# Softmaxes, waiting copies and a DMA queue put in another order: top-k attention and a GELU MLP on one Trainium2 core

## The chip, the cores and the metric
The kernel runs on one core of one Trainium2 chip. The metric is the device time of one execution in microseconds (us), and less is better. The profiles show the core's engines: PE (matmul, with its weight loads as PEld), DVE (vector), ACT (scalar), POOL and SP, whose queue issues the transfers spoken of here. Each engine runs its own instructions in program order.

## The reference
Attention with only the 32 largest scores of each row kept, then an MLP with exact GELU, all in float32.

```python
# q, k, v: 8 batches, 8 heads, 576 rows, 64 dims
scores = 1 / sqrt(64) * q @ k.T
kth    = 32nd largest of each row
scores = where(scores >= kth, scores, -1e9)
scores = scores - max(scores)
attn   = exp(scores); attn = attn / (sum(attn) + 1e-9)
x      = (attn @ v), heads side by side       # 4608 x 512
out    = gelu_exact(x @ w_in) @ w_out         # 512 x 2048, 2048 x 512
```

## The kernel before
The attention is cut into 144 *items*, 18 for each batch. Two heads make a pair, four pairs a batch. A main item is one pair and one tile of 128 rows (four tiles of a pair). The remaining 64 rows of a head go into *last-row items*, each for two pairs. In even batches the two last-row items come at the end of the batch, in odd ones at its start, so that over each two batches four of them follow one another (items 88 to 91, for instance). `starts` holds the first item of each batch.

The main loop has one *slot* n for each item and works on several items at once, in stages. In slot n:

- PE computes scores of item n + 2, and in most even slots those of n + 3 as well (`scores`, L406, L421); ACT copies them out of PSUM (L414, L425).
- DVE finds the 32 largest scores of item n (`top_k`, L502 and L505, after `larger`, L441).
- POOL writes the threshold (`threshold`, L516 and L517), and ACT softmaxes item n - 1: `select`, an activation that pushes scores below the threshold far down (L536), and `softmax`, the exponential with its sum (L548), once for each of the two heads e = 0, 1. Then POOL adds the 1e-9 (`add_small`, L529), DVE inverts (`inverse`, L523), and POOL normalises (L571).
- PE transposes item n - 2 (`transposes`: L371, L385, L647, L661), with ACT's copies of the results (keys: L379, L390; L650; `pt`: L676).
- PE multiplies item n - 3 by v (`attend`, L727, and L738 for last-row items), and `copy_x` lets ACT copy the result into xT (L732, L744).
- PE's pieces of the MLP (`mlp`) fill in: h_ps (L790), in odd slots followed by ACT's two gelus (`run_gelus`, L806, with a table load ahead), and the products with w_out (L944, L946), whose copies ACT makes (L965, L962). Every fourth pair of slots closes a block of 256 tokens, with more copies by ACT (L987 to L1003).

Scores, threshold, softmax and the rest of an item thus run through slots that follow one another, and what each engine does in a slot is set by the order in which the loop calls these functions. In a slot before the change ACT's order is: score copies, then `copy_x` (L1222), then in odd slots the gelus (with the table load ahead and L965 behind them), then `softmax(n - 1, 0)`, the copies of keys and pt, and `softmax(n - 1, 1)`. A call of `softmax` for an item whose `select` was not yet done does that first. The loop's form holds from slot 13 on (`few[0]`), `late` from slot 11.

In PSUM, o, t_ps, tp_t and seven share one bank, s_ps and tp another, and h_ps and the second s_ps a third: PE's next use of a bank follows ACT's copy of the one before.

Some items (`squared`: from 26 on the even ones, and the last-row items but for the very last) are not transposed on PE alone: DVE transposes blocks (`square_p`), SP writes them to DRAM (`write_p`, L605, four DMAs) and reads them back rearranged into pt (`read_p`, L615, four DMAs). A `delayed` item is a squared last-row item. SP's queue carries these writes and reads, the loads of q, k and v (v: L138 and L142) and the stores of y (`run_stores`, L861). It is ordered by hand: while `held[0]` is set, `issue` puts a load off until `flush` at the end of the slot's `write_p`; `soon` holds one that `issue_soon` lets go after a later attend.

Of the kernel before, what the change touches and what calls it, by code (L numbers as in the profile page):

```python
# [14 lines left out]
def kernel(  # L15
# [239 lines left out]
    items, starts = [], []  # L255
# [19 lines left out]
    few = [False]  # L275
# [305 lines left out]
    def delayed(i):  # L581

        return squared(i) and items[i][1] == NM
# [23 lines left out]
    def read_p(i):  # L607

        if squared(i):
            d = turned.pop(i)  # L610
            if i % 2 == 0:
                pt_now[0] = pt_tile()
            cols = slice(i % 2 * P, (i % 2 + 1) * P)
            for k in range(P // SQ):
                nc.sync.dma_start(  # L615
                    out=pt_now[0][k * SQ : (k + 1) * SQ, :, cols], in_=d[:, :, k, :]
                )
# [77 lines left out]
    def copy_x():  # L695
        while copies:
            copies.pop()()
# [10 lines left out]
    def attend(i):  # L708

        if i < 0 or i >= N:  # L710
            return False
        pair, t = items[i]
        b, at = divmod(pair, NP)
        if t < NM and t % 2 == 0:
            return False
        pt = pt_now[0]
        o = bank("o")
        n, row = (2 * P, (t - 1) * P) if t < NM else (TL, SM)
        tok = place_of(b, row)
        gap = RING if t == NM else COLS if tok % RING >= COLS else RING - COLS  # L720
        assert read[0] >= tok - gap + n
        c = slice(column(tok), column(tok) + n)
        if t < NM:
            vt = raw_of("v", pair)
            for j in range(NJ):
                for e in range(2):
                    nc.tensor.matmul(  # L727
                        o[e * D : (e + 1) * D, 0:n], lhsT=vt[:, j, e, :],
                        rhs=pt[:, e * NJ + j if j < NM else NM, :],
                        start=(j == 0), stop=(j == NJ - 1),  # L730
                    )
            copies.append(lambda: nc.scalar.copy(out=xT[:, at, c], in_=o[:, 0:n]))  # L732
        else:
            for r in range(2):
                vt = raw_of("v", pair + r)
                for j in range(NJ):
                    for e in range(2):
                        nc.tensor.matmul(  # L738
                            o[e * D : (e + 1) * D, r * TL : (r + 1) * TL],
                            lhsT=vt[:, j, e, :],  # L740
                            rhs=pt[:, e * NJ + j if j < NM else NM, i % 2 * P :][:, half(r, e)],
                            start=(j == 0), stop=(j == NJ - 1),
                        )
            copies.append(lambda: nc.scalar.copy(  # L744
                out=xT[:, at : at + 2, c],
                in_=o[:, 0 : 2 * TL].rearrange("p (r n) -> p r n", n=TL),
            ))

        if t == (NM if b % 2 == 0 else NM - 1):
            for r in range(2 if t == NM else 1):  # L750
                f = lambda r=r: load("v", pair + r + NP)
                if r == 0 and delayed(i):
                    soon.append(f)
                else:
                    issue(f)
        if at == (NP - 1 if t < NM else NP - 2):
            assert n_tok[0] == tok
            n_tok[0] = tok + n
        return True
# [106 lines left out]
    def run_stores():  # L866
        for f in older:
            f()
        older[:] = stores
        stores.clear()  # L870
# [303 lines left out]
    for n in range(ahead):  # L1174

        held[0] = n < N and squared(n - 2)
        mid = [i for i in (n - 5, n - 4) if delayed(i) and n % 2 and (i % 2 or i in starts)]
        even_last = delayed(n - 4) and n % 2 == 0 and n - 4 not in starts
        if not mid and not even_last:
            read_p(n - 3)  # L1180

        def mids():
            attend(mid.pop(0))
            if not mid:
                copy_x()
                read_p(n - 3)
                issue_soon()
        left[0] = room_in(n)
        few[0] = n > START + 2
        eager[0] = n > N  # L1190
        left[0] += closes(n - 3) - closes(n - 2)
        if not waits(unit_in(n)):
            weights_add(unit_in(n))
        if n > 0:
            larger(n + 1)
        for piece in squares_in.pop(n, []):
            piece()
        if n == 1:

            for e in range(2):  # L1200
                select(0, e)
            for e in range(2):
                softmax(0, e)
        two = few[0] and n % 2 == 0 and n + 3 < N and items[n + 3][1] < NM
        scores(n + 2, two)
        if two:
            scores(n + 3)
        if even_last:
            product = attend(n - 4)
            issue_soon()  # L1210
            read_p(n - 3)
        else:
            product = not delayed(n - 3) and attend(n - 3)
        if len(mid) == 2:
            mids()
        late = n > START
        if n != 1 and n < START:

            for e in range(2):
                select(n - 1, e)  # L1220
            softmax(n - 1, 0)
        copy_x()  # L1222
        if n == START:

            for e in range(2):
                select(n - 1, e)
            softmax(n - 1, 0)
        if waits(unit_in(n)):
            weights_size(unit_in(n))
            weights_add(unit_in(n))  # L1230
        mlp(1)
        if closes(n - 3):
            ready[0] = n_tok[0]
        if few[0] and n % 2:
            run_gelus()
        tr = transposes(n - 2)
        if product and n > START and done[0] < len(pieces) and pieces[done[0]][0] > ready[0]:

            for piece in tr[:1]:
                piece(n + 2 if few[0] else None)  # L1240
            tr, ready[0] = tr[1:], n_tok[0]
        if not few[0] and n > START:
            softmax(n - 1, 0)
        mlp(1)
        if n != 1 and not late:
            softmax(n - 1, 1)
        if few[0]:
            softmax(n - 1, 0)
            if n % 2:
                mlp(ODD)  # L1250
                if mid:
                    mids()
        mlp(1)
        prep = prep_in.pop(n, [])
        if n == 0:
            weights_size(unit_in(1))
            keep_busy(14, ident)
        if n == START + 1:

            for piece in prep:  # L1260
                piece(None)
            prep = []
        if len(prep) > 1 and len(tr) == 3:
            tr, prep = tr[:1] + prep[:1] + tr[1:], prep[1:]
        now = tr[:-1]
        if few[0]:
            now, tr, prep = tr + prep[:1], [], prep[1:]
        for x, piece in enumerate(now):
            piece(n + 2 if few[0] else None)
            ready[0] = n_tok[0]  # L1270
            if few[0] and x == 2:
                break
            mlp(1)
        ready[0] = n_tok[0]
        if late:
            softmax(n - 1, 1)
        if n > 0:
            smaller(n + 1)
        add_small(n - 1)
        for piece in tr[-1:] + prep:  # L1280
            piece(None)
            mlp(1)
        if n < START:

            keep_busy(4 if n == 0 else 8 if product else 14 if n < 5 else 18, ident)

        run_gelus()
        mlp(left[0])
        run_gelus()
        if n < N:  # L1290
            top_k(n, lambda: inverse(n - 1), lambda: square_p(n - 2))
            write_p(n - 2)
            flush()
            if n == 0:
                larger(1)
        else:
            inverse(n - 1)
        threshold(n)
        if n == 0:
            smaller(1)  # L1300
        normalise(n - 1)
        sum_up(n + 2)
        if n in sums_in:
            weight_sums(sums_in[n])
        run_small(6)

        if n > 0 and not waits(unit_in(n + 1)):
            weights_size(unit_in(n + 1))
        run_stores()
        if n == N:  # L1310
            run_stores()
        for m in (n + 1, n + 2):

            if m > 2 and waits(unit_in(m)) == (m == n + 1):
                load_weights(m)
        if n < NP:
            load("v", n)
        if n == 5:
            nc.vector.memset(flat["k"][0][TL:, 0:TL], 0.0)
            load("q", SQUARES)  # L1320
            load("k", SQUARES)
# [38 lines left out]
```

## Time and profile before

| | |
|---|---|
| time, median of 3 runs | 1477.53 us (1476.33 to 1479.15) |
| the profiled execution: its time, its span | 1479.29 us, 1477.5 us |
| granted TensorE clock | 0.999 |
| busy share of the span: PE, PEld, DVE, ACT, POOL | 98%, 77%, 89%, 73%, 77% |
| q1 (all of SP's transfers): MB, share of 16 engines | 124.93, 39.8% |
| writes of turned<-s, reads of pt<-turned | 240 each, 144 KB, 3.5 and 3.2 us to landing |
| loads of v, stores of y | 64 of 128 KB (3.0 us), 30 of 256 KB (2.1 us) |

A line of the timeline gives the start in us from the span's start, the duration, the engine (SPq is SP's DMA queue, at the time of issue), the line of the kernel, the operation, what it writes and reads, and a count; in brackets stands the idle time before it on its engine, and what ended that. A line of the waits gives the engine and line that waited, what it waited for, the us in total, how often, and the longest. A number such as 98% is an average over all stages.

### The profile page before, as it was taken

The page shows a single profiled execution, that of the slowest core. Times are in us where ns is not written, and L with a number is a line of the kernel's source. Part 1 is how long each engine was busy: PE and PEld are TensorE (multiplying, and loading weights), DVE is VectorE, ACT ScalarE, POOL GpSimd, SP SyncE. Part 2 cuts the span into 40 slices and gives each one's busy share as a digit, 9 for nine tenths or more (in the row PEclk, how much of TensorE's full clock was granted, in tenths as well). Part 3 has the DMA queues.
Part 4 walks back from the last instruction along what each step waited for, and adds up shares of the span by engine and source line. Part 5 has one row for each costly group of instructions (what it writes and reads, how often), then busy time and mean ns, then how long its engine had stood idle before and what let it go on. Part 6 is the DMA issues. An engine that isn't in the chain of part 4 may idle for free. (4 is left out here: it accounts for less than half of the span.)

```text
span 1477.5 us, 26521 instructions
## 1 busy us (share of the span) xinstructions
PE 1449.7 (98%) x8693; PEld 1134.6 (77%) x8693; DVE 1307.8 (89%) x3331; ACT 1082.8 (73%) x1902; POOL 1142.0 (77%) x1290
## 2 busy tenths in 40 slices
PE   8999999999999998999999999999999999999999
PEld 6776677887777776888777777787777777787787
DVE  7999899999999999899999999899999999898701
ACT  7999877877777686777777777677777777677620
POOL 6877567878898888777898978787788888887632
PEclk9999999999999999999999999999999999999999
DMA  7425210045435356345534347344543435523300
GB/s 198 144 86 129 78 47 1 24 92 103 93 71 91 67 107 129 65 95 112 102 81 78 74 74 151 76 92 96 99 101 73 89 63 97 125 61 73 68 15 15
DMA packets 544713, 127.04 MB, mean 86 GB/s; under 512 B 466464, under 2 KB 536128, under 8 KB 544576
## 3 DMA queue, kind: packets, MB, share of 16 engines
q1 hardware_dynamic: 543312, 124.93, 39.8%
q8 instruction: 69, 1.13, 0.3%
q14 instruction: 68, 0.56, 0.1%
q10 hardware_dynamic: 1200, 0.39, 0.1%
q0 software_dynamic: 64, 0.03, 0.0%
HBM read 80.47 MB, written 44.83 MB: 85 GB/s over the span
## 5 line engine op out<-in xcount | busy, mean ns | idle before, releaser
L790 PE MATMUL h_ps<-xT,w_in_sb 128*128 128x256 f32 (+1 forms) x2560 | 534.1, 361 | 0.0
L790 PEld LDWEIGHTS h_ps<-xT,w_in_sb 128*128 128x128 f32 x2560 | 437.5, 190 | 73.3 <-issue 25.2
L502 DVE MAX8 top<-lists 128x8 f32<-128x576 f32 (+1 forms) x792 | 475.5, 639 | 0.0
L505 DVE MATCH_REPLACE8 lists<-top,lists 128x288 f32<-128x288 f32 (+1 forms) x528 | 307.6, 588 | 0.0
L571 POOL TENSOR_TENSOR s<-s,stat 128x1152 f32<-128x1152 f32 x135 | 286.1, 2119 | 0.3 <-DVE stat L523 0.3
L536 ACT ACTIVATE s<-s,stat 128x576 f32<-128x576 f32 x288 | 224.7, 788 | 16.6 <-POOL stat L516 16.4
L548 ACT ACTIVATE s<-s,stat 128x576 f32<-128x576 f32 x288 | 224.6, 782 | 11.3 <-POOL lists L466 0.7
L529 POOL TENSOR_SCALAR stat<-stat 128x2 f32<-128x2 f32 x144 | 31.6, 219 | 210.4 <-ACT s L548 183.8
L474 POOL TENSOR_TENSOR lists<-lists 128x576 int32<-128x576 int32 x132 | 186.4, 1412 | 4.0
L466 POOL TENSOR_TENSOR lists<-s 128x576 int32<-128x576 int32 x133 | 188.0, 1413 | 0.0
L727 PE MATMUL o<-pt,raw_v 128*64 128x256 f32 x1280 | 152.9, 384 | 4.3 <-DMA pt<-turned 2.4
L806 ACT ACTIVATE g<-h_ps 128x512 f32<-128x512 f32 x144 | 78.2, 594 | 107.0 <-PE h_ps L790 106.8
L727 PEld LDWEIGHTS o<-pt,raw_v 128*64 128x64 f32 x1280 | 87.9, 136 | 88.3 <-issue 43.1
L946 PE MATMUL y_ps<-w_out_sb,sum 128*128 128x256 f32 x472 | 140.8, 380 | 0.0
L414 ACT ACTIVATE s<-s_ps 128x1024 f32<-128x1024 f32 x127 | 124.9, 1031 | 9.2 <-PE s_ps L406 8.8
L406 PE MATMUL s_ps<-kt,qm 64*128 64x512 f32 x512 | 129.4, 618 | 0.8 <-ACT s L412 0.8
L676 ACT COPY pt<-tp 128x1024 f32<-128x1024 f32 x73 | 74.4, 1019 | 56.2 <-PE tp L661 56.1
L505 DVE MATCH_REPLACE8 lists<-first,lists 128x288 f32<-128x288 f32 x264 | 114.2, 438 | 0.0
L946 PE MATMUL y_ps<-w_out_sb,g 128*128 128x256 f32 x480 | 113.4, 379 | 0.0
L523 DVE RECIPROCAL stat<-stat 128x2 f32<-128x2 f32 x144 | 22.9, 159 | 95.2 <-POOL stat L529 94.4
L502 DVE MAX8 first<-lists 128x8 f32<-128x288 f32 x268 | 106.5, 436 | 0.0
L441 DVE TENSOR_TENSOR lists<-s 128x576 f32<-128x576 f32 x133 | 101.1, 760 | 0.0
(162 smaller groups left out, 2483.3 us busy)
## 6 DMA issues: line engine op xcount, KB each, us to landing
turned<-s SPq DMA_DIRECT2D x240, 144.0 KB, 3.5
pt<-turned SPq DMA_DIRECT2D x240, 144.0 KB, 3.2
raw_v<-in_v_dram SPq DMA_DIRECT2D x64, 128.0 KB, 3.0
raw_q<-in_q_dram SPq DMA_DIRECT2D x112, 72.0 KB, 2.3
raw_k<-in_k_dram SPq DMA_DIRECT2D x112, 72.0 KB, 2.4
out_dram<-y SPq DMA_DIRECT2D x30, 256.0 KB, 2.1
w_out_sb<-in_moe_w_in_dram SPq DMA_DIRECT2D x14, 511.8 KB, 4.8
w_out_sb<-in_moe_w_out_dram SPq DMA_DIRECT2D x10, 511.8 KB, 4.1
```

The source lines that it names most:

```text
L406: nc.tensor.matmul(s_ps[:, e], lhsT=q_t[rows, :], rhs=kt[rows, main_keys(pair)], start=True, stop=True)
L414: nc.scalar.activation(spread(s, S + TL, SM), s_ps, func=AF.Copy, scale=scale)
L466: nc.gpsimd.tensor_tensor(t[:, :, 1].bitcast(i32), a.bitcast(i32), b.bitcast(i32), op=ALU.add)
L474: nc.gpsimd.tensor_tensor(into_of(i)[:, :, 1].bitcast(i32), both, top, op=ALU.subtract)
L502: nc.vector.max(x[:, e], src[:, e])
L505: nc.vector.match_replace(dst[:, e], x[:, e], src[:, e], LOWEST)
L536: nc.scalar.activation(s, s, func=AF.Prelu, bias=st["neg"][:, e : e + 1], scale=1.0, alpha=STEEP)
L548: nc.scalar.activation(s, s, func=AF.Exp, bias=st["bias"][:, e : e + 1], scale=1.0, accum_out=st["den"][:, e : e + 1],)
L571: nc.gpsimd.tensor_tensor(s, s, wide, op=ALU.mult)
L727: nc.tensor.matmul(o[e * D : (e + 1) * D, 0:n], lhsT=vt[:, j, e, :], rhs=pt[:, e * NJ + j if j < NM else NM, :], start=(j == 0), stop=(j = ...
L790: nc.tensor.matmul(h_tile(u)[:, i, :], lhsT=w_in_sb[:, ko, f * P : (f + 1) * P], rhs=xT[:, ko, c0 : c0 + n], start=(ko == 0), stop=(ko == ...
L946: nc.tensor.matmul(acc[names][:, k], lhsT=lhsT, rhs=rhs, start=(j == 0 and k == 0), stop=(j == FT // 2 - 1 and k == 1),)
```

## The change
From slot 13 on:

- In even slots `select(n - 1, 0)`, `softmax(n - 1, 0)` and `select(n - 1, 1)` come ahead of `copy_x`, and `softmax(n - 1, 1)` right behind it.
- In odd slots both selects come ahead of `copy_x` and of the gelus with their table load; both exponentials follow the gelus and L965, ahead of the copies of keys and pt.
- On SP, at the four last-row items, v's first loads behind an odd one of these items are no longer put off through `soon`, and the stores of y of one slot are issued at the next slot's start, behind its reads. At three places in the kernel (near 575, 920 and 1268 us) the order turns from read (4), write (4), four loads of v, two stores of y, read (4), with four loads of v ahead of the write, into read (4), write (4), eight loads of v, read (4), two stores of y.

PE, DVE and POOL run the same instructions in the same order as before; ACT runs the same ones in another order.

```diff
                 f = lambda r=r: load("v", pair + r + NP)
-                if r == 0 and delayed(i):
+                if r == 0 and delayed(i) and i % 2 == 0:
                     soon.append(f)
                 else:
                     issue(f)
...
+        def stores_later(m):
+            return m % 2 == 0 and delayed(m - 3) and m - 4 in starts
+
         even_last = delayed(n - 4) and n % 2 == 0 and n - 4 not in starts
         if not mid and not even_last:
             read_p(n - 3)
+        if stores_later(n):
+            run_stores()
...
+        if few[0]:
+            select(n - 1, 0)
+            if n % 2 == 0:
+                softmax(n - 1, 0)
+            select(n - 1, 1)
         copy_x()
+        if few[0] and n % 2 == 0:
+            softmax(n - 1, 1)
...
         if few[0]:
-            softmax(n - 1, 0)
             if n % 2:
+                softmax(n - 1, 0)
+                softmax(n - 1, 1)
                 mlp(ODD)
                 if mid:
                     mids()
...
-        if late:
+        if late and not few[0]:
             softmax(n - 1, 1)
...
-        run_stores()
+        if not stores_later(n + 1):
+            run_stores()
```

## The prediction
> **What bounds the kernel now.** I read the page first, then the busy times by window, PE's waits, the waits of all engines, and the timeline at the places that the diff touches.
>
> ```profile
> span 1477.5 us, 26521 instructions
> PE 1449.7 (98%) x8693; PEld 1134.6 (77%) x8693; DVE 1307.8 (89%) x3331; ACT 1082.8 (73%) x1902; POOL 1142.0 (77%) x1290
> ```
>
> The profiled execution took 1479.29 us, 1.76 us over the median of 1477.53. All that follows is a difference of times, so I add it to the median. The window is two batches of the regular part (584 to 932 us); its columns are the length and then the busy time of PE, PEld, DVE, ACT, POOL.
>
> ```profile
> 584.00:932.00 348.00, 342.64 (x2041) 269.33 (x2037) 326.30 (x835) 256.61 (x457) 286.99 (x322) 1.00 0.47 93
> ```
>
> PE is the bound, and DVE is close behind: over the 18 pairs of slots in this window DVE has 21.7 us left, 1.2 us a pair. What the change can win is what PE waits for. PE's waits from 120 us on are short: engine, line, releaser, us in total, times, longest.
>
> ```profile
> PE o L738 <- DMA pt<-turned: 5.7, 3, 2.2
> PE o L727 <- DMA pt<-turned: 2.4, 2, 1.9
> PE t_ps L371 <- ACT xT L744: 2.2, 3, 0.7
> PE tp_t L647 <- POOL s L571: 1.5, 4, 0.5
> PE o L727 <- ACT s L548: 1.2, 1, 1.2
> ```
>
> Together 13.0 us, 0.9% of the span: that is all there is to win. What the change visibly acts on lies beside PE:
>
> ```profile
> POOL stat L529 <- ACT s L548: 183.8, 71, 6.0
> ACT g L806 <- PE h_ps L790: 106.8, 52, 11.7
> DVE stat L523 <- POOL stat L529: 94.4, 91, 9.8
> ```
>
> POOL and, through it, DVE wait for ACT's exponentials, while ACT stands at the head of its queue waiting for PE's h_ps. With the selects and exponentials put ahead of those waits, most of the 94.4 us of DVE goes. DVE is not the bound, so this is worth nothing by itself. What it can buy is a lead of the thresholds over PE.
>
> **Part 1: ordinary pairs of slots.** In an odd slot ACT ran gelu's table load, two gelus and the copy L965, then the first select. Now both selects come first, and they need POOL's L516 of the same slot.
>
> ```profile
> 806.63 0.79 POOL L516 TENSOR_SCALAR stat<-top 128x2 f32<-128x2 f32 x1 [0.60 <-DVE stat L523]
> 806.83 1.09 ACT L806 ACTIVATE g<-h_ps 128x512 f32<-128x512 f32 x2 [2.04 <-PE h_ps L790]
> 807.80 0.38 ACT L965 COPY p<-seven 128x256 f32<-128x256 f32 x1
> 810.08 0.38 PE L371 MATMUL tp_t<-kt,qm 128*128 128x128 f32 x2
> ```
>
> L516 ends at 807.42, 0.59 us after h_ps was ready for the gelu (806.83). Call the time from L516's end to h_ps the lead: here it is −0.59. After the change the gelu cannot start before L516's end + 0.80 + 0.86 (two selects) + 1.30 (table load; it no longer lies inside the wait for h_ps), 2.96 in all; the durations are those of the rows at 845 us below. PE is touched when the copy L965 is late for tp_t, which takes the same PSUM bank: L965 ends at 808.18, tp_t starts at 810.08, so 1.9 us are free. PE loses nothing from a lead of 1.1 us on (2.96 − 1.9). With today's lead it would lose 1.6 us, once; that stall itself lifts the lead to 1.1, and the waits of DVE that go (94.4 over 91, about 1 us a slot) lift it further. I charge nothing per slot and keep the 1.6 us for a rival.
>
> In an even slot select, exponential, select now stand before the copy of o into xT.
>
> ```profile
> 815.41 1.95 ACT L414 ACTIVATE s<-s_ps 128x1024 f32<-128x1024 f32 x2
> 818.32 0.37 ACT L732 COPY xT<-o 128x256 f32<-128x256 f32 x1 [0.96 <-PE o L727]
> 820.89 0.38 PE L371 MATMUL t_ps<-kt,qm 128*128 128x128 f32 x2
> ```
>
> The score copies end at 817.36; 0.80 + 0.87 + 0.86 later is 819.9, so the copy ends near 820.3 in place of 818.69, and t_ps (same bank) starts at 820.89. Cover 0.6 us, price 0. If the threshold came over 0.6 us later than now, each even slot would pay the excess.
>
> **Part 2: odd slots that begin with a score copy** (two in each of three places where four last-row items follow one another).
>
> ```profile
> 845.02 1.03 ACT L425 ACTIVATE s<-s_ps 128x1024 f32<-128x1024 f32 x1 [1.05 <-PE s_ps L421]
> 846.05 1.28 ACT L806 ACT_TABLE_LOAD   x1
> 847.35 1.08 ACT L806 ACTIVATE g<-h_ps 128x512 f32<-128x512 f32 x2
> 848.32 0.38 ACT L965 COPY p<-seven 128x256 f32<-128x256 f32 x1
> 848.57 0.80 ACT L536 ACTIVATE s<-s,stat 128x576 f32<-128x576 f32 x1
> 849.40 0.45 PE L385 MATMUL tp_t<-kt 128*64 128x64 f32 x8
> 849.43 1.28 ACT L548 ACT_TABLE_LOAD   x1
> 850.73 0.78 ACT L548 ACTIVATE s<-s,stat 128x576 f32<-128x576 f32 x1
> ```
>
> ACT is busy without a gap here, and the copy at 845.02 waits for PE, so no lead helps. Two selects (1.65) ahead of the load: L965 ends at 848.70 + 1.65 = 850.35 in place of 848.70, and PE's tp_t moves from 849.40 to 850.4: +1.0 us, and again one slot pair later, 2.0 to 2.1 in each place.
>
> [...]
>
> This also fixes when the second of these slots sends out its exponentials.
>
> ```profile
> 864.81 1.02 ACT L425 ACTIVATE s<-s_ps 128x1024 f32<-128x1024 f32 x1 [2.84 <-PE s_ps L421]
> 874.08 0.19 ACT L548 ACTIVATION_READ_ACCUMULATOR s<-s,stat 128x1 f32 x1
> ```
>
> Before: 874.27. After: 864.81 + 1.0 (the stall above) + 1.03 + 0.80 + 0.86 + 1.30 + 0.97 (gelus to L965) + 0.25 + 1.30 + 0.78 + 0.87 + 0.1 = 874.1. So behind this slot POOL and DVE stand where they stood before, and the lead gained in ordinary slots isn't carried to the next step.
>
> **Part 3: the odd slot four items later** (items with transposes through DRAM).
>
> ```profile
> 903.99 0.22 POOL L516 TENSOR_SCALAR stat<-top 128x2 f32<-128x2 f32 x1
> 907.16 0.24 ACT L744 COPY xT<-o 128x128 f32<-128x128 f32 x1
> 907.45 0.49 PE L371 MATMUL t_ps<-kt,qm 128*128 128x128 f32 x2 [0.74 <-ACT xT L744]
> ```
>
> PE's t_ps waits for the copy L744 already now, 3.24 us after L516's end (904.21). The order was select, load, exponential, L744. It becomes select, select, load, gelus, copy L962, load, exponential, exponential, L744: 0.03 + 0.80 + 0.86 + 1.30 + 0.97 + 0.25 + 1.30 + 0.78 + 0.87 + 0.29 = 7.4, so t_ps at 911.6. That is 4.1 us later than in the trace, three times: **+12.3 us**. The stalls of part 2 lie inside it, since PE only comes earlier to the same wait; so does today's 0.74.
>
> **Part 4: SP's queue behind it.** The last-row items' writes, the loads of v, the stores of y and the reads go through one queue.
>
> ```profile
> 912.11 3.39 SPq L605 DMA_DIRECT2D turned<-s  x4
> 918.71 1.29 SPq L861 DMA_DIRECT2D out_dram<-y  x2
> 920.11 3.33 SPq L615 DMA_DIRECT2D pt<-turned  x4
> 926.13 1.39 PE L738 MATMUL o<-pt,raw_v 128*64 128x64 f32 x40 [2.25 <-DMA pt<-turned]
> 934.81 2.38 PE L727 MATMUL o<-pt,raw_v 128*64 128x256 f32 x20 [0.52 <-DMA pt<-turned]
> ```
>
> With the stores behind the reads these leave 1.4 us earlier (920.11 − 918.71); the eight loads of v are the same eight, four of them now behind the write. PE comes 4.1 us later. So 2.25 at L738 is covered by 4.1 alone: the waits of L738 (5.7) go, and L727's 1.9 with them. The 0.5 at 934.81 I leave: a read for it must follow the attend that is itself 4 us later. **−7.6 us.** The move of the stores has 2 us of cover behind it and no reader, price 0. Note that it would have won these 5.7 to 7.6 us on its own: they are hidden by part 3's wait, not added to it.
>
> **Part 5: the rest.** From the first changed slot to the second score copy of the first batches there is one short stretch:
>
> ```profile
> 128.21 1.02 ACT L676 COPY pt<-tp 128x1024 f32<-128x1024 f32 x1
> 129.84 1.09 PE L421 MATMUL s_ps<-kt 64*64 64x512 f32 x8
> ```
>
> L676 ends at 129.23 with 0.6 us free before L421, which takes its bank; behind the second select and exponential (0.86 + 0.87) it ends 1.7 us later, and 0.8 more if the first select holds the gelus up too: 1.1 to 1.9 us, of which I take **+1.4 us** (0 if PE has been held up before). The four waits tp_t <- POOL s (1.5) and the one at the end for an exponential (1.2) go, as POOL and ACT run earlier there: **−2.7 us**, 0 at the worst.
>
> Sum: 12.3 + 1.4 − 7.6 − 2.7 = +3.4 us: 1477.53 + 3.4 = **1480.9 us**. A measurement of this kernel can tell about 0.2%, 3 us, from no change, so this case lies on that border. Its own range: +1 (no first stretch, and part of part 3 won back by an earlier L516) to +6 (the last 2.7 not won), 1478.5 to 1483.5.
>
> **The rivals.**
> *The lead holds where it is needed (faster).* If DVE and POOL, freed of the 94.4 us, put L516 of part 3's slot 4.1 us ahead of 904.2, t_ps doesn't wait at all; then SP's order pays too. All 13.0 us go, part 2 (3 × 2.1) and 1.4 remain: −5.3, 1472.2 us; with part 2 covered as well, 1466. It decides between 1 us of lead (nothing) and 4 us (all). For it: POOL and DVE lose far more than 4 us to ACT between 875 and 904. Against: the 874.1 above, and DVE's 1.2 us a pair.
> *The lead is never built (slower).* The selects become ready only when h_ps is about ready, so that ACT's wait changes its name, and the gelu follows h_ps by 2.96 + 0.6. Then PE loses 1.6 us in each of the four ordinary stretches (6.4), and as much again if DVE and POOL fall back in the slots where a block of tokens ends: 1477.53 + 3.4 + 6.4 = 1487.3, at worst 1493.7. It decides at a lead of 1.1 us. For it: −0.59 now, and 1.2 us a pair is a thin reserve. Against: the waits of DVE for exponentials that go.
> [...]
>
> **How the numbers follow.** The forecast 0.42, split by its place on the border: 0.02 faster, 0.20 within 0.2%, 0.20 slower. Lead holds 0.28: 0.26 faster, 0.02 within. Lead never built 0.27: 0.25 slower, 0.02 within. Longer loads 0.03, slower. In sum faster 0.28, same 0.24, slower 0.48. The range goes from 1470 (a third of the faster rival is below it, 0.09) to 1489 (a third of the slower one and the longer loads above, 0.12).
>
> **What would show it.** In the changed profile DVE's wait for L529 falls from 94.4 us to under 40; ACT's wait of gelus for h_ps shrinks from 106.8 and that of selects for L516 grows. PE shows t_ps <- L744 of 3 us or more three times, tp_t L385 <- the copy L965 of about 1 us, and no L738 <- DMA. I am wrong if t_ps in those three slots doesn't wait (the faster rival), if tp_t or h_ps waits for ACT in most odd slots (the slower one), or if load to gelu takes over 2 us.

## The result and the profile after

The changed kernel takes 1491.48 us, median of 5 (1491.01 to 1493.45), against 1477.11 us, median of 5, of the kernel before on the same chip: 1.0100 of it, with an interval of 1.0086 to 1.0113. That is 14.4 us more. It was forecast slower, by 3.4 us; the measured time lies above the stated range. The profiled executions are closer to one another, 1491.33 and 1479.29 us, since that of before was 2.2 us over its median; their spans differ by 12.0 us, which is what can be looked up in the traces.

The first lines of the page after, and the same window of two batches (length; PE, PEld, DVE, ACT, POOL; granted clock):

```profile
span 1489.5 us, 26645 instructions
PE 1455.8 (98%) x8693; PEld 1137.3 (76%) x8693; DVE 1330.9 (89%) x3331; ACT 1066.1 (72%) x1902; POOL 1138.6 (76%) x1290
```

```profile
584.00:932.00 348.00, 339.96 (x1960) 265.69 (x1960) 330.06 (x821) 247.12 (x449) 281.74 (x320) 0.99 0.45 89
```

PE is as busy as before by this number, 98%, and the kernel is slower all the same: for the same 8693 matmuls PE is busy 6.1 us longer, part of it at a lower clock. The 1960 matmuls of this window in place of 2041 overstate the loss, since the work has moved within it: moved along by 12 us (596 to 944 us) the window holds 2011. PE's waits after, from 120 us on:

```profile
PE o L738 <- ACT y L962: 10.3, 3, 4.4
PE tp_t L385 <- ACT p L965: 3.7, 6, 0.6
PE o L727 <- DMA pt<-turned: 2.8, 3, 1.2
PE tp_t L371 <- ACT p L965: 1.3, 3, 0.4
PE s_ps L421 <- ACT pt L676: 0.8, 1, 0.8
```

Every wait for a copy that stands behind gelus (L962, L965) is new. And what the change visibly acted on:

```profile
DVE stat L523 <- POOL stat L529: 69.1, 66, 6.2
POOL stat L529 <- ACT s L548: 153.1, 67, 5.4
ACT g L806 <- PE h_ps L790: 56.3, 20, 11.7
ACT s L536 <- POOL stat L516: 117.9, 44, 6.8
```

DVE's wait fell from 94.4 to 69.1 us, not under 40. ACT's wait for h_ps halved and its wait for thresholds rose to 117.9: at the head of ACT's queue one wait has taken the other's place.

I set the two traces' PE instructions side by side, one by one (they are the same 8693 in the same order), and read off where the second falls behind. The *lag* is how much later an instruction starts in the second trace. Lost, in us of the span: 1.0 near 130 us; nothing in the ordinary slots (the lag is 4.23 us at 615 and 4.20 at 749 us); then in each of the three places of the four last-row items, from the first score copy to L738's second wait, 5.1, 8.4 and 5.3, of which 1.9, 1.4 and 2.9 come back by 600, 950 and 1300 us; at the end 1.8 come back. 1.0 + 18.8 − 6.1 − 1.8 = 11.9, and 0.1 is drift in the ordinary slots.

The second of the three places in the timeline after, against the rows at 904 to 907 us of before:

```profile
910.85 0.22 POOL L516 TENSOR_SCALAR stat<-top 128x2 f32<-128x2 f32 x1
911.11 1.44 ACT L536 ACTIVATE s<-s,stat 128x576 f32<-128x576 f32 x2 [6.79 <-POOL stat L516]
912.56 1.28 ACT L806 ACT_TABLE_LOAD   x1
913.86 1.08 ACT L806 ACTIVATE g<-h_ps 128x512 f32<-128x512 f32 x2
914.83 0.38 ACT L962 COPY y<-seven 128x256 f32<-128x256 f32 x1
915.26 2.40 PE L738 MATMUL o<-pt,raw_v 128*64 128x64 f32 x40 [4.43 <-ACT y L962]
918.06 0.24 ACT L744 COPY xT<-o 128x128 f32<-128x128 f32 x1
919.46 0.64 PE L371 MATMUL t_ps<-kt,qm 128*128 128x128 f32 x2
```

ACT stood idle for 6.8 us, waiting for the threshold; for the last 2.9 of them PE had finished the h_ps that the gelus behind it need (L790 ends at 908.2). Then two selects and the table load pass before the gelus. The wait isn't where I had put it: o of L738 goes into the bank that `seven` holds until L962 has copied it, so PE stops at L738 (4.4 us here, 2.9 at each of the other two places), and t_ps 4 us later doesn't wait any more.

One more thing is new. The same 40 matmuls of L738 took 1.39 us before and take 2.40 here. Single microseconds of the window view show why (the third number from the end is the granted clock):

```profile
913.00:914.00 1.00, 0.00 (x0) 0.00 (x0) 1.00 (x5) 0.99 (x2) 1.00 (x2) 1.00 0.16 34
915.00:916.00 1.00, 0.74 (x14) 0.74 (x16) 1.00 (x1) 0.98 (x2) 1.00 (x3) 0.50 0.00 0
920.00:921.00 1.00, 1.00 (x4) 0.82 (x4) 0.16 (x1) 0.28 (x1) 0.92 (x2) 0.53 0.73 204
921.00:922.00 1.00, 1.00 (x6) 0.43 (x7) 0.95 (x3) 0.00 (x0) 0.92 (x4) 1.00 1.04 248
```

From 914.1 us, late in the stall, the clock stands at 0.5 for 6.8 us; behind the two shorter stalls it does so for 3.4 us. Lined up with before, the instructions in these stretches take 2.3, 1.3 and 1.4 us longer.

### The profile page after: what moved, and what is told of

Its sections match the earlier page's. It is cut to its first block, busy times and chain, and to the rows that moved or that the text cites. A ratio compares the mean times of both kernels' runs of the same rounds, so it can differ in the third digit from the quotient of the medians.

```text
span 1489.5 us, 26645 instructions
## 1 busy us (share of the span) xinstructions
PE 1455.8 (98%) x8693; PEld 1137.3 (76%) x8693; DVE 1330.9 (89%) x3331; ACT 1066.1 (72%) x1902; POOL 1138.6 (76%) x1290
## 4 chain that ended last, share of the span: by engine, by line
PE 69%; POOL 9%; ACT 6%; DVE 3%; issue 2%; DMA 2%; SPq 1%; POOLq 0%; DVEq 0%; ACTq 0%
PE h_ps L790 25%; PE y_ps L946 15%; PE o L727 8%; PE s_ps L406 5%; PE tp L661 4%; PE seven L944 2%; PE y_ps L908 2%; PE y_ps L911 2%; POOL s L571 2%; ACT s L536 2%; POOL lists L474 1%; PE y_ps L890 1%; DMA pt<-turned 1%; ACT L806 1%; DVE top L502 1%
## 5 line engine op out<-in xcount | busy, mean ns | idle before, releaser
L790 PE MATMUL h_ps<-xT,w_in_sb 128*128 128x256 f32 (+1 forms) x2560 | 534.1, 361 | 0.0
L790 PEld LDWEIGHTS h_ps<-xT,w_in_sb 128*128 128x128 f32 x2560 | 437.5, 190 | 73.3 <-issue 13.1
L536 ACT ACTIVATE s<-s,stat 128x576 f32<-128x576 f32 x288 | 214.7, 775 | 118.0 <-POOL stat L516 117.9
L571 POOL TENSOR_TENSOR s<-s,stat 128x1152 f32<-128x1152 f32 x135 | 286.5, 2122 | 0.3 <-DVE stat L523 0.3
L548 ACT ACTIVATE s<-s,stat 128x576 f32<-128x576 f32 x288 | 223.4, 779 | 6.5
L466 POOL TENSOR_TENSOR lists<-s 128x576 int32<-128x576 int32 x133 | 194.5, 1463 | 0.0
L727 PE MATMUL o<-pt,raw_v 128*64 128x256 f32 x1280 | 152.9, 384 | 3.4 <-DMA pt<-turned 2.8
L727 PEld LDWEIGHTS o<-pt,raw_v 128*64 128x64 f32 x1280 | 87.5, 136 | 87.7 <-issue 44.1
L441 DVE TENSOR_TENSOR lists<-s 128x576 f32<-128x576 f32 x133 | 123.8, 931 | 9.9 <-ACT s L379 7.4
L516 POOL TENSOR_SCALAR stat<-top 128x2 f32<-128x2 f32 x144 | 37.9, 263 | 82.7 <-DVE stat L523 71.3
```

Of the source, the lines that this page charges most:

```text
L466: nc.gpsimd.tensor_tensor(t[:, :, 1].bitcast(i32), a.bitcast(i32), b.bitcast(i32), op=ALU.add)
L536: nc.scalar.activation(s, s, func=AF.Prelu, bias=st["neg"][:, e : e + 1], scale=1.0, alpha=STEEP)
L548: nc.scalar.activation(s, s, func=AF.Exp, bias=st["bias"][:, e : e + 1], scale=1.0, accum_out=st["den"][:, e : e + 1],)
L571: nc.gpsimd.tensor_tensor(s, s, wide, op=ALU.mult)
L727: nc.tensor.matmul(o[e * D : (e + 1) * D, 0:n], lhsT=vt[:, j, e, :], rhs=pt[:, e * NJ + j if j < NM else NM, :], start=(j == 0), stop=(j = ...
L790: nc.tensor.matmul(h_tile(u)[:, i, :], lhsT=w_in_sb[:, ko, f * P : (f + 1) * P], rhs=xT[:, ko, c0 : c0 + n], start=(ko == 0), stop=(ko == ...
```

## The experiments

Each run is given as its ratio to the kernel before on the same chip, with a 95% interval. Where a diff says so it starts from the changed kernel, otherwise from before.

**The queue edits alone** (the two hunks on `soon` and `run_stores`, ACT as before).

> The kernel before with the queue edits alone (eight loads of v behind the write, stores of y behind the reads), ACT in its old order. Theory A (all of the loss comes from ACT's order): the waits of L738 for DMA, 5.7 us in before, mostly go, and with them the half clock near 1275 us: 1471 to 1475 us. Theory B (the moved loads or stores are late for somebody): 1477 us or more, with L727 or L738 waiting for raw_v or pt.

Measured: 1.0009 (1.0001 to 1.0018). No gain.

```profile
PE o L727 <- DMA pt<-turned: 5.2, 4, 1.9
PE tp_t L371 <- ACT xT L744: 2.8, 3, 1.4
PE o L738 <- DMA pt<-turned: 0.6, 1, 0.6
```

L738's 5.7 us are down to 0.6 as the edits intend, but L727, one item later, rises from 2.4 to 5.2, and tp_t waits 2.8 us for the copy L744. The wait was moved along, not removed. Theory A falls for the time, though its mechanism at L738 is there. What theory B named came true: over 1477 us, with L727 waiting for pt.

**ACT's order alone** (the changed kernel with those two hunks taken back).

> The changed kernel with the queue in its old order: ACT's new order alone. Theory A: the stalls of L738 behind the copy L962 and the half clock behind them are all there; 1490 to 1494 us, since PE comes so late that the reads in the old order wait little. Theory B (the queue edits cost part of it): 1480 to 1486 us.

Measured: 1.0065 (1.0051 to 1.0079). So most of the loss comes with ACT's order, as theory A has it, and the queue edits cost some 5 us on top, which it did not allow for. In this trace L738 waits 2.9 us for L962 at all three places; the 4.4 of the changed kernel is missing. Side by side with it, the changed kernel's PE loses 3.9 us, and 3.2 of them at the second place alone. Ahead of that place DVE, POOL and ACT run alike to 0.2 us in both, up to one DVE instruction, L441, which stands before the next thresholds in DVE's order; here are its row and POOL's L571, first in this run and then in the changed kernel:

```profile
888.72 0.76 DVE L441 TENSOR_TENSOR lists<-s 128x576 f32<-128x576 f32 x1
889.49 2.10 POOL L571 TENSOR_TENSOR s<-s,stat 128x1152 f32<-128x1152 f32 x1
```

```profile
889.27 2.11 POOL L571 TENSOR_TENSOR s<-s,stat 128x1152 f32<-128x1152 f32 x1
889.33 2.66 DVE L441 TENSOR_TENSOR lists<-s 128x576 f32<-128x576 f32 x1 [0.27 <-DVE stat L523]
```

Started behind L571, L441 takes 1.9 us longer here (the last section has more of these), the next threshold comes 2.3 us later, and the longer stall is followed by twice the time at half the clock. So in these two traces most of what the queue edits cost on top comes from this, not from a transfer that PE waits for. Why L441 started 0.3 us later stays open. It does so in the two runs with added matmuls too, but not in `old_mid` and `old_mid_copy` below, which have the same queue edits.

**Second exponential behind the copies of keys and pt again** (from the changed kernel).

```diff
         copy_x()
-        if few[0] and n % 2 == 0:
-            softmax(n - 1, 1)
...
                 softmax(n - 1, 0)
-                softmax(n - 1, 1)
                 mlp(ODD)
...
-        if late and not few[0]:
+        if late:
             softmax(n - 1, 1)
```

> The changed kernel, but the second exponential stands behind the copies of keys and pt again, as in before; both selects and the first exponential stay in the new place. Theory A: no L441 of DVE above 1.5 us (14 of 2.1 to 2.7 us in the changed kernel); the stall near 911 us falls from 4.5 to about 2.6 us; 1487 to 1490 us. Theory C (DVE's 22.7 us of longer L441 are what PE loses): 1478 to 1482 us. If L441 stays long, its cause is another than the copy L379 behind both exponentials.

Measured: 1.0220 (1.0206 to 1.0234): 18 us slower than the changed kernel, where both theories had expected a gain. The first is a group of L441 in the changed kernel, the second the same group here, and then come PE's waits here:

```profile
L441 DVE TENSOR_TENSOR lists<-s 128x576 f32<-128x576 f32 x133 | 123.8, 931 | 9.9 <-ACT s L379 7.4
```

```profile
L441 DVE TENSOR_TENSOR lists<-s 128x576 f32<-128x576 f32 x133 | 101.2, 761 | 0.0
```

```profile
PE o L738 <- ACT y L962: 9.7, 3, 3.2
PE tp_t L371 <- ACT p L965: 8.4, 12, 1.1
PE tp_t L371 <- ACT y L962: 7.2, 6, 1.2
```

The long L441 are gone with the second exponential back behind L379, and the loss isn't, so they are not what PE loses in general. In their place stands what the prediction called the lead that is never built: tp_t in ordinary slots waits for L965 and L962, 15.6 us in 18 waits. With the second exponential late, thresholds come late, and each gelu behind two selects holds PE. So in the changed kernel it is the early second exponential that keeps the ordinary slots free.

**Filling the stall** (from the changed kernel; 24 and then 12 matmuls of 128 columns whose results nobody uses, in a free bank).

```diff
         def mids():
+            if len(mid) == 1 and mid[0] == n - 4 and mid[0] + 1 in starts:
+                warm = pair_tile("warm", "pr")
+                for _ in range(24):
+                    nc.tensor.matmul(warm[:, 0, 0:P], lhsT=ident, rhs=ident, start=True, stop=True)
             attend(mid.pop(0))
```

> The changed kernel with 24 more matmuls of 128 columns on PE (results unused) ahead of L738 in each of the three places where it waits 3.0 to 4.5 us for the copy L962. Theory A (PE's idle time brings the clock down): no half clock at these places, the stall itself the same; 4 to 5 us less, 1486.5 to 1488 us. Theory D (the clock falls for another reason): 1491 to 1493 us with the clock at 0.5 as before.

> The changed kernel with 12 unused matmuls (2.7 us at full clock by the run with 24, whose 24 took 5.4 us and so more than the stalls they were to fill) ahead of L738 in the three places. Theory A (PE's idle time halves the clock): no half clock behind the three places, the stalls as long as before; 3 to 5 us less than the changed kernel's 1.0100 of before, so 1.007 to 1.008. Theory D (the clock falls for another reason): 1.010 or more and the clock at 0.5 there.

Measured: 1.0145 (1.0131 to 1.0159) with 24; these took 5.4 us at each place, more than the stall, and say nothing of the price. With 12: 1.0091 (1.0077 to 1.0104). The same 20 us of the changed kernel, and with 12 matmuls (each of the 12 counts twice in the trace, so 24 of the 34 more are theirs):

```profile
905.00:925.00 20.00, 15.57 (x93) 12.12 (x93) 18.19 (x47) 9.86 (x16) 19.52 (x24) 0.83 0.60 122
```

```profile
905.00:925.00 20.00, 17.59 (x127) 14.21 (x126) 18.16 (x47) 11.65 (x20) 19.52 (x24) 1.00 0.67 134
```

PE's waits of the run with 12:

```profile
PE t_ps L371 <- ACT xT L744: 2.4, 4, 0.6
PE seven L944 <- ACT xT L744: 1.0, 3, 0.3
PE o L727 <- DMA pt<-turned: 4.0, 3, 1.8
```

The clock stays at 1.00 at all three places (1.000 over the whole profiled run), so it was PE's idle time that brought it down. But the time is within the interval of the changed kernel's 1.0100, where both theories had named another time or another clock: what PE does faster it waits for right afterwards, at t_ps and `seven` for L744, and at L727 for pt. The low clock shows 5 us in the comparison of instructions and is worth nothing that these runs can tell. My reading of the waits is that ACT's chain behind the threshold sets the pace there. It fits that t_ps now waits for L744 at all three places, 0.65 us each, and starts 7.3 us behind the threshold's end each time.

**The old order where the loss shows**, in three steps (from the changed kernel; `old` brings the old order to the odd slots named).

```diff
+        old = few[0] and n % 2 == 1 and (delayed(n - 4) and n - 3 in starts)   # part 3's slots
+        # then: ... or (n + 2 < N and items[n + 2][1] == NM)                    # and score-copy slots
+        # then: bool(mid) or (n + 2 < N and items[n + 2][1] == NM)              # and all attends of last-row items
...
-        if few[0]:
+        if few[0] and not old:
             select(n - 1, 0)
...
                 softmax(n - 1, 0)
-                softmax(n - 1, 1)
+                if not old:
+                    softmax(n - 1, 1)
...
-        if late and not few[0]:
+        if late and (old or not few[0]):
             softmax(n - 1, 1)
```

> The changed kernel with ACT's old order in three slots alone, the ones of part 3, where L738 waits for L962. Theory A (the loss is made at these three places): the stalls of 3.0 to 4.5 us at L738 and the half clock behind them, 15 us in all, are gone, 2 to 4 us of waits for pt come back; 1479 to 1483 us where before is 1478. Theory E (the late thresholds show somewhere else in PE then): 1486 us or more.

Measured: 1.0072 (1.0059 to 1.0084). L962 is no longer waited for, but

```profile
PE seven L944 <- ACT xT L744: 12.7, 3, 4.2
```

stands in its place one odd slot later, where the selects of the new order are ahead of L744. Theory E: the late threshold shows at the next copy.

> As the run before, and ACT's old order also in the odd slots that begin with a score copy (part 2; two in each place, three in the first stretch). Theory A: the six waits of tp_t L385 for L965 (0.6 to 0.7 us each) and the 0.9 at 130 us go as well: 5 us less than the run before, 1474 to 1478 us, so that what is left of the change gains 1 to 4 us over before. Theory E: no less than the run before.

Measured: 1.0072 (1.0060 to 1.0085); 13.1 us at the same place. The six waits of tp_t L385 have gone, and nothing is gained: `seven` waits for L744 behind them as long as before.

> The changed kernel with ACT's old order in every odd slot in which a last-row item is scored or attended, so that the slot behind those of part 3 is old as well (there the selects stood ahead of the copy L744, for which seven L944 waited 4.4 us when only part 3's slots were put back). Theory A (the loss is made in the slots of the last-row items alone): no wait of PE for L962, L965 or L744 above 1.5 us there, no half clock; 1476 to 1481 us where before is 1478. Theory H (whatever is put back, the next late copy takes its place, since the thresholds come late): 1485 us or more, with a stall of 3 us or more somewhere near 580, 930 and 1280 us.

Measured: 1.0019 (1.0010 to 1.0027). With that slot old as well, no wait for L962 or L744 is left in the list (2.3 us for L965 are), and 8.1 thousandths, some 12 us, of the change's loss are gone. The largest wait left is the one below; its longest, 3.3 us, is again followed by half the clock (near 591 us).

```profile
PE o L727 <- DMA pt<-turned: 8.4, 3, 3.3
```

A run with the old order in all odd slots (the new one in even slots and the queue edits left) had been expected at 1475 to 1479 us if odd slots alone make the loss, and at 1484 or more if even slots then suffer, with t_ps and h_ps waiting for L732. It took 1484.55 us, 1.0038 (1.0026 to 1.0051), but not by those waits: its longest item is L727 <- DMA pt<-turned, 10.3 us in 4 waits.

**Gelus first** (from the changed kernel: in odd slots gelus and L965 ahead of both selects, the two exponentials still together).

> The changed kernel with gelus and their copy ahead of both selects in odd slots; both exponentials still stand together ahead of the copies of keys and pt. Theory A (the selects ahead of the gelus are the whole fault): no wait for L965 or L962, 1.7 us more at t_ps in each of the three places (second select and exponential ahead of L744), 1473 to 1480 us. Theory G (the longer L441 of DVE cost PE time too): 1484 us or more with t_ps or tp_t waiting for ACT in ordinary slots.

Measured: 1.0015 (1.0006 to 1.0024). One exchange in odd slots takes back 8.5 thousandths of the change's loss; no L962 or L965 in PE's list and no clock below 1 but at the end. The selects ahead of the gelus are the fault. The two exponentials ahead of L744 still cost something: t_ps and tp_t wait 7.0 us for it, in place of 2.2 before.

> Gelus ahead of the selects in all odd slots, both exponentials together in ordinary slots, and the old order in the odd slots of last-row items; even slots and the queue as in the change. Theory A: no wait for L965, L962; the waits s_ps L421 and L406 for L676 (2.8 and 1.4 us in the run with gelus first) go in the old-order slots; 1473 to 1478 us. Theory H: no less than the run with gelus first, 1.0015 of before.

Measured: 1.0003 (0.9993 to 1.0012).

> The run before with the queue in its old order. If the queue edits help once ACT is not late: 1 to 3 us more than the run before, with L738 waiting for pt. If they only move the wait from L738 to L727, as they did alone: the same within 1 us.

Measured: 0.9979 (0.9971 to 0.9988), faster than before. So the queue edits cost 2.4 thousandths, 3.5 us, here too, which neither of the two expectations had. The third place with the edits and without (the queue's issues, and L727):

```profile
1270.77 1.02 SPq L861 DMA_DIRECT2D out_dram<-y  x2
1271.89 4.14 SPq L605 DMA_DIRECT2D turned<-s  x4
1278.75 2.54 SPq L615 DMA_DIRECT2D pt<-turned  x4
1284.15 2.38 PE L727 MATMUL o<-pt,raw_v 128*64 128x256 f32 x20 [2.35 <-DMA pt<-turned]
```

```profile
1270.05 3.46 SPq L605 DMA_DIRECT2D turned<-s  x4
1276.29 2.54 SPq L615 DMA_DIRECT2D pt<-turned  x4
1281.59 2.38 PE L727 MATMUL o<-pt,raw_v 128*64 128x256 f32 x20 [0.64 <-DMA pt<-turned]
```

Put behind one item's reads, the stores stand ahead of the next item's write. The write leaves 1.8 us later, of which the two stores fill 1.1, and takes longer to issue; its read leaves 2.5 us later, and L727 starts 2.6 us later. PE was 0.9 us behind just ahead of this L727 in any case, so the wait cost 1.7 us here.

> The run with gelus first and old last-row slots, of the queue edits the loads of v alone; y's stores ahead of the reads as in before. Theory S (the stores, put behind the reads, stand ahead of the next write L605 and hold it and the reads behind it): the reads for L727 near 930 us leave 1 to 2 us earlier than with both edits; 0.997 to 0.9985 of before. Theory L (the loads cost it): 0.9995 to 1.001.

> The same with the stores' edit alone. Theory S: L727 waits 5 to 8 us for pt in all, 0.9995 to 1.0015 of before. Theory L: 0.997 to 0.9985, with L727's waits at 2 to 3 us.

Measured: loads alone 0.9983 (0.9975 to 0.9992), stores alone 0.9993 (0.9985 to 1.0002), with L727 at 2.2 and 8.6 us in PE's waits:

```profile
PE o L727 <- DMA pt<-turned: 2.2, 2, 1.4
```

```profile
PE o L727 <- DMA pt<-turned: 8.6, 3, 3.6
```

The wait belongs to the stores, as theory S says. In the profile with the stores alone PE falls 5.8 us behind at the three places; that execution lies 3.2 us above its run's median. In time the intervals of the two touch, so that the stores cost more than the loads is likely and not shown; together they cost 2.4 thousandths.

> Old queue, old even slots, old last-row slots; in ordinary odd slots gelus first, then both selects, both exponentials, and the copies behind. If the gain comes from the earlier second exponential of odd slots: 0.997 to 0.9985. If from even slots: 0.9995 to 1.001.

> Old queue, all odd slots old, even slots in the new order. If the gain comes from even slots: 0.997 to 0.9985, with no wait at the end of the kernel for L548 (1.2 us in before). If from odd slots: 0.9995 to 1.001; if the late second exponential of odd slots makes the early selects of even slots late: over 1.002.

Measured: odd part alone 0.9973 (0.9962 to 0.9983), even part alone 1.0012 (1.0004 to 1.0021). What gains is one thing: in ordinary odd slots both exponentials together, behind gelus and L965 and ahead of the copies. This version, 1476.04 us against 1479.68 on its chip, beats both kernels. Its ACT in the slot that the prediction showed at 806 us:

```profile
806.50 1.09 ACT L806 ACTIVATE g<-h_ps 128x512 f32<-128x512 f32 x2 [2.04 <-PE h_ps L790]
807.48 0.38 ACT L965 COPY p<-seven 128x256 f32<-128x256 f32 x1
807.73 1.46 ACT L536 ACTIVATE s<-s,stat 128x576 f32<-128x576 f32 x2
809.21 1.28 ACT L548 ACT_TABLE_LOAD   x1
```

The gelus keep their place at h_ps, and the selects fit behind them. Side by side with before, PE gains 2.2 us at the four waits of tp_t for POOL's s, 0.9 at the end, and 1.4 where before's clock is at half near 1275 us; it loses some 1 us each at a score product near 131 us and twice at reads of pt.

## Why the prediction was right and wrong

*What bounds the kernel:* right. PE has 13.0 us to win at most, and the best version won 3.6.

*Part 1, ordinary slots at nothing:* right. The lag doesn't change there, and the run with the second exponential put back shows on what that rests: without it, PE pays at tp_t, 18 us in the measured time. The rival "lead never built" was a true mechanism; the changed kernel isn't in it.

*Part 2, 1.0 us in each slot that begins with a score copy:* the mechanism and the six places are right, the size was 0.62 to 0.7; two selects in a row take 1.44 us (the row at 911.11), where the sum has 1.65. That the first stretch costs 1.4: measured 1.0.

*Part 3, 12.3 us:* the chain was right, the place of the wait was not: not t_ps behind L744 but L738 behind L962, which I had in the chain and did not check against PE's next use of its bank. From the first score copy to t_ps and without the low clock the lag grew by 3.8, 6.1 and 3.9 us, for the 4.1 each of the prediction. From the threshold's end to t_ps the prediction counts 7.4 us, and with the clock held (12 matmuls) it was 7.3 at each place, with t_ps waiting for L744. L516 came 1.35, 6.86 and 11.69 us later than before, and of that 1.0, 4.2 and 11.3 are PE's own lag ahead of the place; so the first and third threshold stood within 0.4 us of where the prediction had anchored them. The second came 2.6 us later than that. DVE's L441 took 2.66 us there in place of 0.76; I count 1.9 of the 2.6 to it, and the run with ACT's order alone bears that out: with 0.76 there its second stall is 2.9 us like the others.

*The failed steps.* The larger one by size is part 3's neighbourhood: parts 2 and 3 came to 18.8 us in place of 12.3. I priced the one slot in which a wait stood already, kept the threshold where it stood, and no step asked what a PE idle for 3 us does next. The second threshold was 2.6 us late, and the comparison by instruction shows 5.0 us at half the clock, which the prediction lacks. The run that held the clock shows that the low clock by itself is not what made the time, since L744 and pt were waited for in its place: behind t_ps the prediction ends, and `seven` and L727 wait there. That this step fails without the queue edits is seen in ACT's order alone, 1.0065, some 9.6 us.

Part 4 is the other, and it is wrong in kind. It gave the queue edits −7.6 us, by way of part 3's cover, and put the stores' move at nothing, "2 us of cover behind it and no reader". I looked at who reads the stores, not at what is queued behind them: the next write, its read, and L727. In the changed trace 6.1 us come back at the three places, and 1.4 of these are there because before ran a stretch near 1275 us at half the clock. In four pairs of runs the edits cost 0.9 to 3.5 thousandths (alone, behind gelus first, with old odd slots 1.0038 against 1.0012, and 1.0100 against 1.0065). The 3.5 of the last pair come for the most part by L441's late start, as said there, so that the other three, 0.9 to 2.6, speak for the queue. The statement that they would win 5.7 to 7.6 us alone is refuted by the first run. And of part 5's −2.7 us 1.8 came: the wait at the end went, three of the four waits of tp_t for POOL became waits for L965.

*Against the sum:* forecast +3.4, span +12.0. Of the 8.6 between, 6.5 lie in parts 2 and 3 (18.8 for 12.3: by the instructions, the low clock 5.0, the second place 2.0, the other two −0.5), 1.5 in part 4, 0.9 in part 5, −0.4 in the first stretch, and 0.1 is drift. Of the other 2.4 us up to the measured 14.4, 2.2 are the profiled execution of before, which was that far above its median.

*Longer loads, 0.03 of the forecast:* no run shows a load that holds ACT for longer than its row says. All 136 loads of the trace after have 1.28 us, as the 136 of before, and load to gelu takes 1.30 us here too (912.56 to 913.86), where it now stands in the path with the gelu's input long ready.

## What to carry to other kernels

When instructions that wait for a slow chain are put ahead of ones that wait for the bound engine, list every buffer that the passed copies free, and check each against the bound engine's next use of it: here the gelus' copy, not the obvious one, held the bank. Here moving work earlier paid where the moved instruction sat behind the bound engine's copies and ahead of idle time (the second exponential of odd slots, 0.9973), and cost where it sat ahead of them (the selects ahead of the gelus: 1.0100, and 1.0015 with the gelus first). In a queue, ask what a moved transfer now stands in front of, and don't sum a term by a stall that another term is about to hide.

## What the runs showed of the hardware

PE's clock halved after some of PE's short idle times. In the changed kernel the stalls of 2.9 to 4.4 us were each followed by 0.5 of the clock, for 3.4 us or for 6.8, and 12 matmuls put into the stall kept it at 1.00. One idle time of 2.2 us in the kernel before had the same effect near 1274 us, another of 2.25 us at 924 us had none. Longer ones without effect stand in other runs: 3.1 us ahead of L738 at 926.6 in the fastest version, 3.2 at 567.9 with the second exponential put back. Over all the traces, from 120 to 1470 us, the clock fell in the idle time or within 3.5 us behind it at 11 of 11 idle times of PE above 3.25 us, at 7 of 10 from 2.9 to 3.25, and at 4 of 18 from 2.0 to 2.9. So one idle time of 2.2 us had the half clock behind it here, and one of 3.2 us had not; what decides between them these traces don't show.

DVE's L441 and, after it, POOL's L466 are slow where L441 starts behind POOL's L571. In the trace after, L441 takes 0.76 us where it starts ahead of POOL's L571, and 2.1 to 2.7 us where it starts behind it:

```profile
625.32 2.11 POOL L571 TENSOR_TENSOR s<-s,stat 128x1152 f32<-128x1152 f32 x1
625.35 2.69 DVE L441 TENSOR_TENSOR lists<-s 128x576 f32<-128x576 f32 x1 [0.23 <-ACT s L379]
627.39 1.92 POOL L466 TENSOR_TENSOR lists<-s 128x576 int32<-128x576 int32 x1
```

L466, POOL's next, is then slow in its turn: 1.92 us behind these L441, 1.40 at 119 of the other 120. In 12 of 13 such cases L441 came too late by waiting for ACT's copy L379, which it needs and which the change put behind both exponentials (7.4 us in 14 waits; here it comes 0.03 us too late). The thirteenth is the one at 889.33 us. All thirteen began 0.02 to 0.60 us behind L571's start and ended 0.61 or 0.62 us behind its end, whenever they had begun. The thirteen gave DVE 21.6 us more, and most of them lie in ordinary slots, where PE lost nothing; that DVE had the time to spare is my reading of it. The one at 889.33 us came ahead of a threshold that PE's stall hung on.
